# The last head's output weights: a quarter moved to two small loads, most of it on three DMA engines, ahead in the queue

## The chip, the cores and the metric

One core of a Trainium2 chip. The metric is the device time of one execution in microseconds (us), the median of several executions. Times inside an execution are counted from the start of the profiled span, which is some 1.7 us shorter than the device time.

A *row* below is one row of the output weights (512 bf16, 1 KB). The *rows step* is the group of small matmuls that reorders the attention outputs for the output product, and the *output matmuls* are those of that product. A *hole* is a stretch in which TensorE stands still with no semaphore to wait for. A *block* is 256 TensorE instructions: in the trace before, the holes end at instructions 450, 706, 962, 1218 and 1986, all multiples of 256 apart, with 0.4 to 1.1 us idle in each, and each ends 2.16 to 2.44 us after the start of an instruction packet of 16,384 B. At two more multiples, 1474 and 1730, there is no hole. *V4* is the load of the V rows of KV head 4; heads count from 0. An *increment* is one step of a load's semaphore, which counts up as the DMA engines of the load finish (the prediction reads it so; the load of V5 shows 16 of them in the trace before, from 55.51 to 57.26 us).

## The reference, cut to what matters

```python
# B=4 tokens, D=512, 32 query heads, 8 KV heads, head size 128, window of 1024 of 4096 positions
xn = layernorm(x)
q  = xn @ wq                                        # 512 x 4096
o  = softmax(q @ k.T * 128**-0.5) @ v               # per KV head: 1024 positions, 4 batches
s  = o.reshape(B, 1, 4096) @ wo                     # wo: 4096 x 512, 512 rows for each KV head
g  = silu(gelu(layernorm(xn) @ w1 + b1) @ w2 + b2)
return x + s * g
```

Almost everything is read once: 8 MB of K, 8 MB of V, 4 MB of each of wq and wo, 3.5 MB of MLP weights.

## The kernel before

All loads are issued in one queue, in the order in which they are used: wq and K, then V with the MLP weights between, then wo. What the change touches is at the end.

```python
wo_r = A_wo.rearrange("(g p i) o -> p g i o", g=HKV, i=4)   # head g: partition p holds 4 rows
for n, (g0, g1, i0, i1) in enumerate(((0, 2, 0, 4), (2, 4, 0, 4), (4, 6, 0, 4), (6, 7, 0, 4),
                                      (7, 8, 0, 3), (7, 8, 3, 4))):
    ...  # six loads; the last head's come as 3 + 1 rows of each partition

def to_rows(g0, g1):                  # 16 matmuls with selectors: OTb (head dim on partitions)
    ...                               # -> OW (rows on partitions, the order of the loads)
    t = add("pe", fn, ep[g1 - 1], c_sel, ex[HKV - 2])    # ep: the last head's epilogue
    return add("dve", ... OW[:, :, g0*4:g1*4] <- psx ..., t)

def wo(k, rows):                      # per head and row of the partition: 4 matmuls, 128 x 128 by 4
    ...
    last = pe.matmul(psM[:, PS_W + c * 4:PS_W + (c + 1) * 4],
                     wo_sb[:, g, i, c * 128:(c + 1) * 128], OW[:, i, g * 4:(g + 1) * 4], ...)
    return add("pe", fn, d, rows, mlp["g"])

for g in range(HKV):
    PV(g)                             # P times V on TensorE, then a matmul for the sums
    ...                               # epilogue(g - 1), parts of the MLP
epilogue(HKV - 1)
rows = to_rows(0, HKV)
for k in range(len(d_wo)):
    t_w = wo(k, rows)                 # 128 output matmuls; then product, transpose, sum, store
```

The softmax here doesn't subtract the row's maximum and nothing guards it: scores larger than these inputs give would overflow.

## Time and profile before

| Kernel before | |
|---|---|
| device time, median of 3 | 77.0 us (77.0 to 77.06) |
| profiled span | 75.3 us |
| bytes read | 28.85 MB |
| last increments of the last weights' semaphore | 72.17 us |
| hole among the output matmuls, from the last start before it to the next start | 69.38 to 70.13 us |
| product after the output matmuls starts | 72.52 us |

The prediction shows the lines that carry this. The table of stretches: stretch, its length, busy us and number of instructions of TensorE, its weight loads, VectorE, ScalarE and GpSimd, granted clock, DMA share, and in the last column GB/s.

```profile
52.00:54.00 2.00, 0.60 (x24) 0.53 (x21) 0.92 (x2) 0.98 (x2) 0.00 (x0) 0.90 1.00 422
54.00:56.00 2.00, 0.74 (x6) 0.46 (x6) 1.26 (x4) 0.00 (x0) 0.00 (x0) 0.50 1.03 434
56.00:58.00 2.00, 2.00 (x76) 2.00 (x76) 0.96 (x4) 0.18 (x1) 0.00 (x0) 0.50 1.02 430
```

### The profile page before, as it was taken

The page shows a single profiled execution, that of the slowest core. Times are in us where ns is not written, and L with a number is a line of the kernel's source. Part 1 is how long each engine was busy: PE and PEld are TensorE (multiplying, and loading weights), DVE is VectorE, ACT ScalarE, POOL GpSimd, SP SyncE. Part 2 cuts the span into 40 slices and gives each one's busy share as a digit, 9 for nine tenths or more (in the row PEclk, how much of TensorE's full clock was granted, in tenths as well). Part 3 has the DMA queues.
Part 4 walks back from the last instruction along what each step waited for, and adds up shares of the span by engine and source line. Part 5 has one row for each costly group of instructions (what it writes and reads, how often), then busy time and mean ns, then how long its engine had stood idle before and what let it go on. Part 6 is the DMA issues. An engine that isn't in the chain of part 4 may idle for free.

```text
span 75.3 us, 2297 instructions
## 1 busy us (share of the span) xinstructions
PE 50.0 (66%) x1046; PEld 39.8 (53%) x1058; DVE 39.3 (52%) x82; ACT 9.8 (13%) x16; POOL 4.6 (6%) x14
## 2 busy tenths in 40 slices
PE   0000039993859949987997994999069879818770
PEld 0000039992359939976997860104049576518740
DVE  0778107786058967985996424001664679770010
ACT  0611000000090303111130630003300000000000
POOL 6980000000000000000000000000000000000000
PEclk9999999999999999999999999569755555555555
DMA  1899999998999999999999999999999999999600
GB/s 36 244 455 405 420 422 479 435 444 370 427 422 431 422 418 431 427 414 466 401 420 453 406 443 390 427 431 409 427 427 440 418 401 416 418 420 416 252 25 2
DMA packets 4219, 28.99 MB, mean 385 GB/s; under 512 B 493, under 2 KB 625, under 8 KB 1650
## 3 DMA queue, kind: packets, MB, share of 16 engines
q1 hardware_dynamic: 4160, 28.84, 92.2%
q8 instruction: 8, 0.13, 0.6%
q10 hardware_dynamic: 50, 0.01, 0.1%
q14 instruction: 1, 0.01, 0.0%
HBM read 28.85 MB, written 0.00 MB: 383 GB/s over the span
## 4 chain that ended last, share of the span: by engine, by line
DMA 36%; PE 35%; SPq 16%; issue 5%; DVE 4%
DMA wo_sb<-in_A_wo_dram 24%; PE psK L278 22%; SPq L475 15%; DMA kv_buf<-in_A_k_cache_dram 12%; PE psS L297 7%; PE psO L362 3%; DVE kt_buf L284 2%; DVE q_sb L368 1%; PE psK L374 1%; PE psM L507 1%; PE psK L346 1%; PE psS L538 1%; SPq L212 1%; SPq L205 0%; DVE o_bf L540 0%
## 5 line engine op out<-in xcount | busy, mean ns | idle before, releaser
L278 PE MATMUL psK<-ident,kv_buf 128*128 128x128 bf16 x256 | 21.2, 237 | 11.8 <-DMA kv_buf<-in_A_k_cache_dram 10.6
L284 DVE COPY kt_buf<-psK 128x1024 bf16<-128x1024 bf16 x32 | 21.3, 691 | 8.7 <-PE psK L278 8.6
L278 PEld LDWEIGHTS psK<-ident,kv_buf 128*128 128x128 bf16 x256 | 17.1, 108 | 11.1 <-DMA kv_buf<-in_A_k_cache_dram 10.6
L297 PE MATMUL psS<-qT,kt_buf 128*128 128x16 bf16 x256 | 10.4, 169 | 1.7 <-issue 1.1
L297 PEld LDWEIGHTS psS<-qT,kt_buf 128*128 128x128 bf16 x256 | 9.4, 96 | 3.0 <-issue 2.1
L315 PEld LDWEIGHTS psO<-P_buf,kv_buf 128*128 128x128 bf16 x256 | 7.4, 102 | 3.0 <-issue 3.0
L315 PE MATMUL psO<-P_buf,kv_buf 128*128 128x16 bf16 x256 | 8.0, 173 | 1.0 <-DVE OTb L333 0.6
L328 DVE TENSOR_REDUCE den_sb<-psS 128x16 f32<-128x512 f32 x8 | 5.5, 691 | 4.2 <-PE psO L315 4.0
L305 ACT ACTIVATE P_buf<-psS 128x512 bf16<-128x512 f32 x8 | 4.8, 597 | 17.1 <-PE psS L297 17.1
L400 PE MATMUL psK<-w_sb,yT 128*32 128x512 bf16 x16 | 4.9, 1093 | 1.3 <-issue 1.3
L507 PE MATMUL psM<-OW,wo_sb 128*128 128x4 bf16 x128 | 3.9, 166 | 1.1 <-issue 0.6
L507 PEld LDWEIGHTS psM<-OW,wo_sb 128*128 128x128 bf16 x128 | 3.6, 104 | 1.4 <-issue 1.2
L411 DVE SCALAR_TENSOR_TENSOR kt_buf<-kt_buf,psK 128x512 f32<-128x512 f32 x1 | 0.7, 686 | 6.4 <-ACT kt_buf L410 6.4
L534 DVE TENSOR_TENSOR sg_sb<-psM,g_sb 128x16 f32<-128x16 f32 x1 | 0.2, 185 | 4.7 <-PE psM L507 4.7
L400 PEld LDWEIGHTS psK<-w_sb,yT 128*32 128x32 bf16 x16 | 0.5, 114 | 3.8 <-issue 3.8
L369 ACT ACTIVATE q_sb<-psO 128x512 bf16<-128x512 f32 x1 | 0.6, 597 | 13.5 <-PE psO L362 13.5
L424 PE MATMUL psK<-ident,kt_buf 128*128 128x128 bf16 x4 | 0.6, 307 | 2.4 <-DVE kt_buf L419 2.4
L331 DVE RECIPROCAL rden<-den_sb 128x16 f32<-128x16 f32 x8 | 2.0, 253 | 0.3
L362 PE MATMUL psO<-wq_sb,xT 128*32 128x512 bf16 x32 | 1.9, 380 | 0.3 <-DVE xT L351 0.3
L246 DVE CAST P_buf<-x_bf 4x512 f32<-4x512 bf16 x1 | 0.8, 795 | 2.4 <-DMA x_bf<-in_A_x_dram 2.4
L237 POOL TENSOR_SCALAR_AFFINE_SELECT negm<-zero_bf 128x512 bf16<-128x512 bf16 x1 | 1.9, 1852 | 0.1
L321 PE MATMUL psS<-P_buf,ones_bf 128*128 128x512 bf16 x3 | 1.8, 587 | 0.0
(64 smaller groups left out, 27.4 us busy)
## 6 DMA issues: line engine op xcount, KB each, us to landing
kv_buf<-in_A_k_cache_dram SPq DMA_DIRECT2D x8, 1024.0 KB, 19.9
kv_buf<-in_A_v_cache_dram SPq DMA_DIRECT2D x8, 1024.0 KB, 22.8
wq_sb<-in_A_wq_dram SPq DMA_DIRECT2D x2, 2048.0 KB, 11.3
w_sb<-in_B_w_dram SPq DMA_DIRECT2D x2, 1792.0 KB, 27.9
wo_sb<-in_A_wo_dram SPq DMA_DIRECT2D x3, 1024.0 KB, 24.3
wo_sb<-in_A_wo_dram SPq DMA_DIRECT2D x1, 512.0 KB, 21.5
wo_sb<-in_A_wo_dram SPq DMA_DIRECT2D x1, 384.0 KB, 18.2
wo_sb<-in_A_wo_dram SPq DMA_DIRECT2D x1, 128.0 KB, 18.0
```

The costliest lines, as they stand in the source:

```text
L237: c_neg = add("gp", lambda e: e.affine_select(negm[:, :], zero_bf[:, :], [[0, 32], [1, 4], [0, 4]], ALU.is_equal, NEG, base=0, channel_mul ...
L278: last = pe.transpose(psK[n % NB][:, j * 128:(j + 1) * 128], kv_buf[:, g, u * UT + j, :], ident[:, :])
L284: cp[n] = add("dve", lambda e: e.tensor_copy(kt_buf[:, n % NKT, :], psK[n % NB][:, 0:1024]), t, sc.get(n - NKT))
L297: last = pe.matmul(psS[g % 2][:, c * 16:(c + 1) * 16], kt_buf[:, n % NKT, j * 128:(j + 1) * 128], qT[:, g * 16:(g + 1) * 16], start=False, ...
L305: ex[g] = add("act", lambda e: e.activation(P_buf[:, g, :], psS[g % 2][:, 0:512], AF.Exp, scale=SCALE), sc[n])
L315: last = pe.matmul(pso[:, 0:16], kv_buf[:, (HKV + g) % NS, c, :], P_buf[:, g, c * 16:(c + 1) * 16], start=(c == 0), stop=(c == NC - 1))
L328: v = add("dve", lambda e: e.tensor_reduce(den_sb[:, cs], bass.AP(psS[g % 2], 0, [[512, 128], [1, 16], [16, NC]]), AX.X, ALU.add), den[g])
L331: v = add("dve", lambda e: e.reciprocal(rden[:, cs], den_sb[:, cs]), v)
L362: last = pe.matmul(psO[m // 4][32 * s:32 * s + 32, 0:512], xT[:, c, :], wq_sb[:, c, m * 512:(m + 1) * 512], start=(c == 0), stop=(c == 3), ...
L400: pe.matmul(psK[0][32 * s:32 * s + 32, 0:1024].bitcast(F32), yT[:, c, :], bass.AP(w1_sb, c * F + K0[s], [[4 * F, 128], [1, 4], [FC, 128]]) ...
L475: e.dma_start(wo_sb[:, g0:g1, i0:i1, :], wo_r[:, g0:g1, i0:i1, :]))))
L507: last = pe.matmul(psM[:, PS_W + c * 4:PS_W + (c + 1) * 4], wo_sb[:, g, i, c * 128:(c + 1) * 128], OW[:, i, g * 4:(g + 1) * 4], start=firs ...
```

## The change

Some DMA engines end the stream earlier than others, as the semaphores of the loads show (of the last weights' increments in the trace before, eight come by 70.73 us and eight from 71.37 to 72.17). The intent is to give three of the early engines more of the last head's weights and all the others less. So 120 of its 512 rows are loaded by a DMA on 24 partitions, which runs on three engines, and 8 rows by another on 8 partitions. Both come after V4 in the queue and go where the query weights lay. The other 384 rows stay in 128-partition loads. The new layout needs its own selectors, and 24 + 12 output matmuls in place of the last head's 16.

```diff
+    wox_sb = wq_sb[0:24, 0, 0:6 * D].rearrange("p (j o) -> p j o", j=6)
 ...                                    # selectors sel3 and selx, made by GpSimd
+        if g == 4:                     # in the loop over heads, behind load_v(4)
+            R3 = (7 * 512 + 384) * D
+            d_wox = [pg.dma("sp", "wox0", lambda e: e.dma_start(
+                wox_sb[:, 0:5, :].rearrange("p j o -> p (j o)"),
+                bass.AP(A_wo.tensor, R3, [[5 * D, 3], [15 * D, 8], [1, 5 * D]])), t_q),
+                pg.dma("sp", "wox1", lambda e: e.dma_start(
+                    wox_sb[0:8, 5, :], bass.AP(A_wo.tensor, R3 + 120 * D, [[D, 8], [1, D]])), t_q)]
 ...
-    (7, 8, 0, 3), (7, 8, 3, 4)                                # last head: 3 + 1 rows
+    w3_r = A_wo[7 * 512:7 * 512 + 384, :].rearrange("(p i) o -> p i o", i=3)   # 2 + 1 rows
 ...                                    # to_rows: 16 matmuls as before, for heads 0 to 6, and
+            for i in range(3):
+                for j in range(3):
+                    last = pe.matmul(psx[:, 128 + i * 4:132 + i * 4], sel3[:, j, i, :], ...)
+            for a in range(6):
+                last = pe.matmul(psx[0:24, 160 + a * 4:164 + a * 4], selx[:, a, :], ...)
 ...                                    # two more copies by VectorE: OW3, OWx
+        if n == 2:                     # after the third group of output matmuls
+            wo([(wox_sb[:, a, :], OWx[:, a * 4:(a + 1) * 4], False, False) for a in range(5)]
+               + [(wox_sb[0:8, 5, :], OWx[0:8, 20:24], False, False)], rows[2], *d_wox)
```

More of the change, by code (lines that the diff above doesn't have):

```diff
@@ L161, in bass_recurrent_scan__sliding_block_cached__mixer_channel_mlp__decode_kernel @@
     OW = sb([128, 4, HKV * 4], BF16)
+    sel3 = sb([128, 3, 3, 128], BF16)
+    selx = sb([128, 6, 24], BF16)
+    OW3 = sb([128, 12], BF16)
+    OWx = sb([24, 24], BF16)
     hT = sb([128, 64], BF16)
@@ L243, in bass_recurrent_scan__sliding_block_cached__mixer_channel_mlp__decode_kernel @@
         base=0, channel_multiplier=-1), c_o32)
+    ones_w = bass.AP(ones_bf, 0, [[128, 128], [0, 9], [1, 128]])
+    c_sel3 = add("gp", lambda e: e.affine_select(
+        sel3[:, :, :, :], ones_w, [[-128, 3], [1, 3], [3, 128]], ALU.is_equal, 0.0,
+        base=0, channel_multiplier=-1), c_1)
+    c_sx = add("gp", lambda e: e.affine_select(
+        selx[:, 0:5, :], ones_bf[:, 0:120], [[1, 5], [5, 3], [15, 8]], ALU.is_equal, 0.0,
+        base=0, channel_multiplier=-1), c_1)
+    c_sx5 = add("gp", lambda e: e.affine_select(
+        selx[:, 5, :], ones_bf[:, 0:24], [[1, 24]], ALU.is_equal, 0.0,
+        base=120, channel_multiplier=-1), c_1)
     v = add("dve", lambda e: e.tensor_copy(x32[:, :], x_bf[:, :]), d_x)
@@ L466, in bass_recurrent_scan__sliding_block_cached__mixer_channel_mlp__decode_kernel @@
         w2_sb[:, :, :], B_w2.rearrange("(p c) o -> p c o", c=FC)))
-    for g in range(2, HKV):
-        load_v(g)
-    wo_r = A_wo.rearrange("(g p i) o -> p g i o", g=HKV, i=4)
-    d_wo = []
-    for n, (g0, g1, i0, i1) in enumerate(((0, 2, 0, 4), (2, 4, 0, 4), (4, 6, 0, 4), (6, 7, 0, 4),
-                                          (7, 8, 0, 3), (7, 8, 3, 4))):
-        d_wo.append((g0, g1, i0, i1, pg.dma("sp", "wo%d" % n, lambda e, g0=g0, g1=g1, i0=i0, i1=i1:
-                                            e.dma_start(wo_sb[:, g0:g1, i0:i1, :],
-                                                        wo_r[:, g0:g1, i0:i1, :]))))
@@ L478, in to_rows @@
-    def to_rows(g0, g1):
-        psx = psS[0]
-        def fn(pe):
-            last = None
-            for i in range(4):
-                for j in range(4):
-                    last = pe.matmul(psx[32 * j:32 * j + 32, i * 32 + g0 * 4:i * 32 + g1 * 4],
-                                     sel[:, i, :],
-                                     bass.AP(OTb, g0 * 16 + j * 4,
-                                             [[HKV * 16, 128], [16, g1 - g0], [1, 4]]),
-                                     start=True, stop=True)
-            return last
-        t = add("pe", fn, ep[g1 - 1], c_sel, ex[HKV - 2])
-        return add("dve", lambda e: e.tensor_copy(
-            OW[:, :, g0 * 4:g1 * 4],
-            psx[:, 0:128].rearrange("p (i n) -> p i n", i=4)[:, :, g0 * 4:g1 * 4]), t)
@@ L497, in bass_recurrent_scan__sliding_block_cached__mixer_channel_mlp__decode_kernel @@
-    first = [True]
-    def wo(k, rows):
-        g0, g1, i0, i1, d = d_wo[k]
-        def fn(pe):
-            last = None
-            for g in range(g0, g1):
-                for i in range(i0, i1):
-                    for c in range(4):
-                        last = pe.matmul(psM[:, PS_W + c * 4:PS_W + (c + 1) * 4],
-                                         wo_sb[:, g, i, c * 128:(c + 1) * 128],
-                                         OW[:, i, g * 4:(g + 1) * 4],
-                                         start=first[0], stop=(k == len(d_wo) - 1 and i == i1 - 1),
-                                         skip_group_check=True)
-                        first[0] = False
-            return last
-        return add("pe", fn, d, rows, mlp["g"])
@@ L516, in bass_recurrent_scan__sliding_block_cached__mixer_channel_mlp__decode_kernel @@
-    for g in range(HKV):
+    for g in range(HKV):
+        if g >= 2:
+            load_v(g)
+        if g == 4:
[5 more added lines that the diff above has]
+                    wox_sb[0:8, 5, :], bass.AP(A_wo.tensor, R3 + 120 * D, [[D, 8], [1, D]])), t_q)]
@@ L528, in bass_recurrent_scan__sliding_block_cached__mixer_channel_mlp__decode_kernel, with load_wo @@
     epilogue(HKV - 1)
-    rows = to_rows(0, HKV)
-    for k in range(len(d_wo)):
-        t_w = wo(k, rows)
+    wo_r = A_wo.rearrange("(g p i) o -> p g i o", g=HKV, i=4)
+    d_wo = []
+    def load_wo(n, g0, g1, i0, i1):
+        d_wo.append((g0, g1, i0, i1, pg.dma("sp", "wo%d" % n, lambda e: e.dma_start(
+            wo_sb[:, g0:g1, i0:i1, :], wo_r[:, g0:g1, i0:i1, :]))))
+    for n, g0 in enumerate((0, 2, 4)):
+        load_wo(n, g0, g0 + 2, 0, 4)
+    load_wo(3, 6, 7, 0, 4)
+    w3_r = A_wo[7 * 512:7 * 512 + 384, :].rearrange("(p i) o -> p i o", i=3)
@@ new lines, in bass_recurrent_scan__sliding_block_cached__mixer_channel_mlp__decode_kernel, with to_rows, fn @@
+    d_w3 = [(i0, i1, pg.dma("sp", "w3%d" % i0, lambda e, i0=i0, i1=i1: e.dma_start(
+        wo_sb[:, 7, i0:i1, :], w3_r[:, i0:i1, :]))) for i0, i1 in ((0, 2), (2, 3))]
+    def to_rows():
+        psx = psS[0]
+        def fn(pe):
+            last = None
+            for i in range(4):
+                for j in range(4):
+                    last = pe.matmul(psx[32 * j:32 * j + 32, i * 28:(i + 1) * 28],
+                                     sel[:, i, :],
+                                     bass.AP(OTb, j * 4, [[HKV * 16, 128], [16, 7], [1, 4]]),
+                                     start=True, stop=True)
+            o = 7 * 16
+            for i in range(3):
+                for j in range(3):
+                    last = pe.matmul(psx[:, 128 + i * 4:132 + i * 4], sel3[:, j, i, :],
+                                     OTb[:, o + j * 4:o + j * 4 + 4],
+                                     start=(j == 0), stop=(j == 2))
+            for a in range(6):
+                last = pe.matmul(psx[0:24, 160 + a * 4:164 + a * 4], selx[:, a, :],
+                                 OTb[:, o + 12:o + 16], start=True, stop=True)
+            return last
+        t = add("pe", fn, ep[HKV - 1], c_sel, c_sel3, c_sx, c_sx5, ex[HKV - 2])
+        return [add("dve", lambda e: e.tensor_copy(
+            OW[:, :, 0:28], psx[:, 0:112].rearrange("p (i n) -> p i n", i=4)), t),
+            add("dve", lambda e: e.tensor_copy(OW3[:, :], psx[:, 128:140]), t),
+            add("dve", lambda e: e.tensor_copy(OWx[:, :], psx[0:24, 160:184]), t)]
@@ new lines, in wo, with fn @@
+    def wo(tiles, *deps):
+        def fn(pe):
+            last = None
+            for w, o, st, sp in tiles:
+                for c in range(4):
+                    last = pe.matmul(psM[:, PS_W + c * 4:PS_W + (c + 1) * 4],
+                                     w[:, c * 128:(c + 1) * 128], o,
+                                     start=(st and c == 0), stop=sp, skip_group_check=True)
+            return last
+        return add("pe", fn, *deps)
+    rows = to_rows()
+    for n, (g0, g1, i0, i1, d) in enumerate(d_wo):
+        wo([(wo_sb[:, g, i, :], OW[:, i, g * 4:(g + 1) * 4], n == 0 and g == 0 and i == 0, False)
+            for g in range(g0, g1) for i in range(i0, i1)], d, rows[0], mlp["g"])
+        if n == 2:
+            wo([(wox_sb[:, a, :], OWx[:, a * 4:(a + 1) * 4], False, False) for a in range(5)]
+               + [(wox_sb[0:8, 5, :], OWx[0:8, 20:24], False, False)], rows[2], *d_wox)
@@ L534, in bass_recurrent_scan__sliding_block_cached__mixer_channel_mlp__decode_kernel @@
+    for i0, i1, d in d_w3:
+        t_w = wo([(wo_sb[:, 7, i, :], OW3[:, i * 4:(i + 1) * 4], False, i == 2)
+                  for i in range(i0, i1)], d, rows[1])
     v = add("dve", lambda e: e.tensor_tensor(
```

## The prediction

> **What bounds the kernel now.** I read the page first, then the timeline of the last ten microseconds, the chain that ended last, the table of stretches, and last the trace's records of single packets and semaphore increments. Slices, queues and forms, from the page:
>
> ```profile
> PEclk9999999999999999999999999569755555555555
> DMA  1899999998999999999999999999999999999600
> ...
> q1 hardware_dynamic: 4160, 28.84, 92.2%
> q8 instruction: 8, 0.13, 0.6%
> ...
> L507 PE MATMUL psM<-OW,wo_sb 128*128 128x4 bf16 x128 | 3.9, 166 | 1.1 <-issue 0.6
> ```
>
> The DMA row is at nine tenths from 4 us to 70 us, so the kernel is one long stream of transfers (28.84 MB) with a tail. In the packet records the engines are rate bound: an 8,192 B packet takes 309 ns and the next begins 3 ns before its end, 306 ns apart. A megabyte load has eight such packets on each of 16 engines, 2.45 us, and the K loads land 2.45 us apart. The second thing to see is queue 8: eight instruction packets, all 16,384 B, at 25.5, 32.2, 38.3, 44.5, 50.5, 60.6, 67.8 and 71.7 us, each some 0.9 us long. They take time from one data engine at a time.
>
> The semaphore records show what this does. A load counts up as its 16 engines finish. Up to 25 us all increments of one load lie within 0.35 us. After that one more engine falls 1.2 to 1.4 us behind with each instruction packet. The last weight load counts 70.42, 70.47, 70.48, 70.51, 70.62, 70.64, 70.73, 70.73 and then 71.37, 71.82, ... 72.17: eight engines are early and eight late. I followed packets from end to start. The engine that alone carries the 3,584 B packet of b1, a one-row load, is never hit and writes its last data at 70.29 us. Two of the three others among the lowest four (those of the four-row b2 load) are not hit either. This is what the change wants to use.
>
> The end, from the timeline and then from the chain:
>
> ```profile
> 67.19 0.30 PE L486 MATMUL psS<-OTb,sel 128*32 128x32 bf16 x16 [1.30 <-DVE OTb L333]
> 67.56 0.29 DVE L493 CAST OW<-psS 128x128 bf16<-128x128 f32 x1 [0.42 <-PE psS L486]
> 68.00 1.55 PE L507 MATMUL psM<-OW,wo_sb 128*128 128x4 bf16 x53 [0.51 <-DVE OW L493]
> 70.13 2.35 PE L507 MATMUL psM<-OW,wo_sb 128*128 128x4 bf16 x75 [0.58 <-issue]
> 72.52 0.18 DVE L534 TENSOR_TENSOR sg_sb<-psM,g_sb 128x16 f32<-128x16 f32 x1 [4.67 <-PE psM L507]
> ```
>
> ```profile
> 53.69 18.16 DMA wo_sb<-in_A_wo_dram
> 71.86 0.05 issue
> 71.90 0.60 PE psM L507 x16
> ```
>
> The chain says that the load of the last head's first three rows of tiles ended the wait at 71.86 us, and 16 matmuls followed. But the timeline says that TensorE is almost as late. It makes 53 output matmuls, stands still with no semaphore to wait for ("issue") until 70.13 us, and makes 75 more. Single starts are 26.7 ns apart. The 112th matmul started at 71.68 us, so TensorE had only about 0.2 us of slack before the load that the chain blames. Of the 0.75 us hole the table of stretches shows:
>
> ```profile
> 69.40:70.13 0.73, 0.15 (x6) 0.09 (x4) 0.00 (x0) 0.00 (x0) 0.00 (x0) 0.50 1.03 411
> 70.13:71.70 1.57, 1.57 (x59) 1.57 (x58) 0.00 (x0) 0.00 (x0) 0.00 (x0) 0.50 0.50 191
> ```
>
> After the hole TensorE is full (1.57 of 1.57 us, 59 matmuls) while the DMA share has fallen to a half.
>
> I numbered TensorE's instructions in order, twice the weight loads plus the waits since some matmul records are missing. Holes without a releaser end at instructions 450, 706, 962, 1218 and 1986, all multiples of 256 apart. So the hole at 70.13 us is a block of instructions that had not arrived. Its packet began at 67.84 us and TensorE went on 2.29 us later; the four earlier pairs give 2.44, 2.22, 2.16 and 2.37 us.
>
> [...]one data increment for b1 (1 row), four for x and b2, eight for each half of x16. For a source of 3 by 8 rows and 24 partitions this gives three engines.
>
> **The change, part by part.** Transfers first. Packet durations are 46 ns for 1,024 B, 121 for 3,072, 159 for 4,096 and 309 for 8,192; a line through them gives 83 ns for 2,048 and 196 for 5,120 (estimates), each less the 3 ns of overlap.
> - Removed on every engine: 8 x 118 + 8 x 43 = 1.29 us for the last head. Added: 8 x 80 + 8 x 43 = 0.98 us for its 384 rows. Every engine ends 0.31 us earlier, the lowest eight 0.25 us because of a row of the small ninth load.
> - Added on the three lowest engines: 8 x 193 ns = 1.54 us plus 0.04. They end 1.3 us later than before, some 71.7 to 72.0 us in increments, level with the late ones.
> So the last weights should land at about 71.9 us instead of 72.17. By itself this is worth 0.2 to 0.3 us. The loads of V4 to V7 lose nothing: V7 landed at 62.11 us and its matmuls started at 64.45.
>
> TensorE next. Output matmuls become 28 x 4 + 6 x 4 + 3 x 4 = 148 instead of 128: 20 x 26.7 ns = 0.53 us more. The rows step grows from 16 to 31 matmuls; nine new ones load 128 columns and I take them at the same 26.7 ns, 0.24 us, the six of 24 columns at the old 7 ns, 0.04 us. So output matmuls begin at about 68.28 us. VectorE gets two more copies behind the first, needed only much later. GpSimd makes 1,152 + 144 more selector elements; 512 took 1.85 us, so about 4.7 us more, done by about 11 us and used at 67 us: free.
>
> Then the block boundary. It stays at instruction 1986, and what stands before the rows step is unchanged, so the boundary is 15 matmuls earlier in the output stage: after 38 of them rather than 53. TensorE gets there at 68.28 + 38 x 0.0267 = 69.29 us. [...]the packet still starts near 67.84 us and TensorE goes on at 70.13 us. This is my main choice: the hole swallows the 0.28 us of the rows step, but it now has 110 matmuls behind it instead of 75. 110 x 26.7 = 2.94 us, last start at 73.04 us, against 72.32 before: **0.72 us later**. The new load is there long before, the last weights at 71.9, so no DMA wait is left in that stretch. The tail (product, transpose, sum, store) is unchanged. The next boundary, 2242, is not reached: the program ends near 2211.
>
> **Rivals.**
> 1. The designer's: DMA sets the end, TensorE's matmuls hide, and 0.25 us is gained: 76.75 us. For it: the chain blames the load. Against: slack of only 0.2 us, and 35 more matmuls.
> 2. The block comes earlier[...], the hole closes. Then TensorE runs from 68.28 for 148 matmuls: last start at 72.20, gain 0.1 us: 76.9 us.
> 3. [...]the block comes some 0.3 us later, and the loss is 1.0 us: 78.0 us.[...]
> 4. An instruction packet falls on one of the three loaded engines, making it 1.2 us late: data at 73.2 us, 12 matmuls left, also about 1 us lost. One packet of eight matters here and three engines of 16, so unlikely.
>
> **Range and chances.** My main way gives 77.0 + 0.7 = 77.7 us; I give it two thirds, the two faster rivals a quarter together, the slower ones the rest. Middle 77.6 us, range 76.75 to 78.0. Two per cent is 1.54 us: no way named here reaches it, so 0.01 faster, 0.97 within, 0.02 slower.
>
> **What would show it.** Last weight increments near 71.9 us with the lowest engines no longer 1.4 us early; eight instruction packets again, the seventh near 67.8 us; a hole in the output matmuls after about 38, ending near 70.1 us; then 110 matmuls without a wait until about 73.1 us, and VectorE's product behind them rather than behind a load. The prediction is wrong if the hole ends before 69.8 us, if the seventh packet moves, or if matmuls at the end again wait for a load.

The sum came to 0.72 us more for the last output matmul, 77.0 + 0.7 = 77.7 us, with 77.6 us as the middle. But two of its inputs stand as my estimates alone: that the 24-partition load runs on three engines (the trace after then showed three data increments), and that the seventh packet still starts near 67.84 us (it started at 67.92). *Lowest* is my name for the engines that the small loads run on; no view numbers the engines, and that they lie one set inside the other was an estimate too. The trace after bears it out for the new loads: three of the eight 1 KB packets of the 8-row load start 1 to 2 ns after a 5 KB packet of the 24-partition load ends, at 54.48, 54.68 and 55.15 us. That the engine of b1 is never hit is my own following of packet records, in which several packets often fit as the next.

## The result and the profile after

The changed kernel took **77.94 us** (median of 4 runs, 77.68 to 78.04), against 77.03 us for the kernel before beside it. The ratio is 1.0114, 95% interval 1.0087 to 1.014. A ratio is always the mean time of one kernel's fast runs over that of the other's fast runs of the same rounds, so it is not quite the ratio of the medians.

The timeline of the changed kernel (start, length, engine, line, operation, count, and in brackets the idle time before it and what ended it):

```profile
67.14 0.30 PE L533 MATMUL psS<-OTb,sel 128*32 128x28 bf16 x16 [1.30 <-DVE OTb L351]
...
68.46 1.15 PE L559 MATMUL psM<-OW,wo_sb 128*128 128x4 bf16 x38 [0.46 <-DVE OWx L551]
70.26 1.71 PE L559 MATMUL psM<-OW,wo_sb 128*128 128x4 bf16 x58 [0.64 <-issue]
71.90 0.80 PE L559 MATMUL psM<-OWx,wq_sb 24*128 24x4 bf16 x24
72.62 0.91 PE L559 MATMUL psM<-OW,wo_sb 128*128 128x4 bf16 x28
```

The hole is now after 38 matmuls, ends at 70.26 us, and 58 + 24 + 28 = 110 matmuls follow. The chain that ended last says the same, and no load is left in its end:

```profile
69.62 0.64 issue
70.26 3.29 PE psM L559 x110
```

The queue is another matter. The same stretches as before:

```profile
52.00:54.00 2.00, 0.78 (x23) 0.48 (x19) 0.97 (x2) 0.93 (x2) 0.00 (x0) 0.85 1.00 410
54.00:56.00 2.00, 0.79 (x7) 0.51 (x8) 1.26 (x4) 0.00 (x0) 0.00 (x0) 0.50 1.01 319
56.00:58.00 2.00, 2.00 (x78) 2.00 (x78) 0.96 (x4) 0.18 (x1) 0.00 (x0) 0.50 1.03 434
```

From 54 to 56 us the engines are as busy as ever (1.01) but move 319 GB/s in place of 434. In the packet records, 8 KB packets that took 309 ns take up to 660 ns there, 58 of them between 53.4 and 56.1 us. All sixteen increments of V5's semaphore come later than before, the earliest at 56.15 us instead of 55.51, and the last weights land at 72.83 us instead of 72.17. The trace that I had predicted for TensorE was there. The loads, which I had expected to gain 0.25 us, had lost 0.66.

### The profile page after: what moved, and what is told of

Read it like the earlier page. It is cut to its first block, busy times and chain, and to the rows that moved or that the text cites. A ratio compares the mean times of both kernels' runs of the same rounds, so it can differ in the third digit from the quotient of the medians.

```text
span 76.3 us, 2387 instructions
## 1 busy us (share of the span) xinstructions
PE 52.7 (69%) x1093; PEld 40.8 (53%) x1093; DVE 39.3 (52%) x84; ACT 9.8 (13%) x16; POOL 6.5 (9%) x17
## 4 chain that ended last, share of the span: by engine, by line
PE 67%; DMA 12%; DVE 9%; issue 7%; ACT 2%; SPq 1%
PE psK L296 22%; DMA kv_buf<-in_A_k_cache_dram 12%; PE psO L333 8%; PE psS L315 8%; PE psK L418 6%; PE psM L559 6%; PE psS L339 4%; PE psO L380 3%; PE psS L311 3%; DVE kt_buf L302 2%; PE psM L460 2%; PE psK L422 1%; DVE q_sb L386 1%; DVE den_sb L346 1%; DVE kt_buf L437 1%
## 5 line engine op out<-in xcount | busy, mean ns | idle before, releaser
L339 PE MATMUL psS<-P_buf,ones_bf 128*128 128x512 bf16 x8 | 4.3, 534 | 0.0
L311 PE MATMUL psS<-negm,ind 128*128 128x512 bf16 x8 | 3.0, 380 | 0.0
```

Source lines behind the costliest of these rows:

```text
L311: pe.matmul(psS[g % 2][:, 0:512], ind[:, :], negm[:, :], start=True, stop=False, skip_group_check=True)
L339: den[g] = add("pe", lambda pe: pe.matmul(psS[g % 2][:, 0:512], ones_bf[:, :], P_buf[:, g, :], start=True, stop=True), ex[HKV - 2 + g % 2] ...
```

## The experiments

Each kernel ran on one chip beside the kernel before, and those of one batch on the same chip. Batch one: e1 to e4. Batch two: e5 to e7. Batch three: e8 to e10 and the changed kernel again. Last: e11.

| Run | What | Median, us | Range of its runs | Ratio to before | 95% interval |
|---|---|---|---|---|---|
| e1_tensor_alone | TensorE's added work only | 77.09 | 76.97 to 77.87 | 1.0014 | 0.9994 to 1.0034 |
| e2_loads_alone | loads only | 77.57 | 77.33 to 77.60 | 1.0071 | 1.005 to 1.0092 |
| e3_spread12 | small load over 12 engines | 77.72 | 77.57 to 78.28 | 1.0111 | 1.0069 to 1.0153 |
| e4_pad12 | 12 useless matmuls at the start | 77.72 | 77.49 to 77.86 | 1.0094 | 1.0068 to 1.0121 |
| e5_aligned | loads only, on partitions 0 to 11 and 32 to 43 (*aligned*) | 76.98 | 76.94 to 77.02 | 0.9998 | 0.9983 to 1.0013 |
| e6_no8rows | loads only, no 8-row load | 77.66 | 77.58 to 78.02 | 1.0096 | 1.0069 to 1.0122 |
| e7_later | loads only, placed after V7 | 77.46 | 77.38 to 77.70 | 1.0071 | 1.0048 to 1.0095 |
| e8_change_aligned | whole change, aligned | 77.28 | 77.11 to 78.08 | 1.0063 | 1.0024 to 1.0101 |
| e9_tensor_first | e8, reordered, with the pad | 77.08 (fast runs) | 76.92 to 77.66 | 1.0031 | 0.9999 to 1.0063 |
| e10_no_small_loads | loads only, 128 rows left out | 76.80 | 76.66 to 76.86 | 0.9971 | 0.9956 to 0.9986 |
| after_again | the changed kernel | 77.62 | 77.47 to 77.79 | 1.0083 | 1.0067 to 1.0099 |
| e11_balanced | repaired version | 76.74 | 76.62 to 76.81 | 0.9963 | 0.9949 to 0.9977 |

The kernel before had medians of 76.92 to 77.04 us in these batches. All runs were fast but one: e9's profiled execution (78.59 us) was slow and is left out of its row.

### TensorE's work alone (e1)

```diff
 # kernel before, its loads unchanged; in to_rows:
+            for a in range(9):  pe.matmul(psx[:, ...], ident[:, :], OTb[:, 112:116], ...)
+            for a in range(6):  pe.matmul(psx[0:24, ...], ident[:, 0:24], OTb[:, 124:128], ...)
 # and after the third group of output matmuls, adding exact zeros:
+                for a in range(20): pe.matmul(psM[:, ...], wo_sb[:, a // 4, 0, ...], zero_bf[:, 0:4], ...)
```

> The kernel before with all its loads as they were, and only TensorE's added work: 15 useless matmuls in the rows step (9 of 128 columns, 6 of 24), two more copies behind it, and 20 matmuls by zero after the third group of output weights. My theory (TensorE's tail behind the instruction block sets the end): as slow as the changed kernel, 77.8 to 78.1 us; the hole after about 38 output matmuls, ending near 70.2 us, and 110 matmuls behind it without a long wait; last weights still landing near 72.2 us. Rival (the loads on three engines slow the stream and set the end): no change, 77.0 to 77.2 us.

The profiled execution took 77.87 us and shows what I expected, by the chain:

```profile
68.48 1.16 PE psM L518 x38
69.64 0.66 issue
70.30 1.68 PE psM L518 x58
```

But the other four executions took 76.97, 76.98, 77.09 and 77.15 us, as fast as the kernel before. So with the added work one execution was 0.9 us slower and four were not. Only one trace of a run is kept, so no trace shows what was different in those four. The other traces do suggest it. In the traces of before, of after and of e1 the rows step starts at 67.19, 67.14 and 67.14 us; in those of e2, e3 and e4 below it starts at 65.71, 65.90 and 65.92 us. In those runs TensorE's holes of the K phase end earlier. The first hole, at instruction 450, ends at 27.94 us in after and at 26.28 us in e2, where the first instruction packet came at 24.0 and not at 25.7 us. I call the first kind executions with *late blocks* and the second kind with *early blocks*. They are the ends of a range and not two separate kinds: in the 13 traces of fast runs the first instruction packet starts between 21.55 us (after_again) and 25.69 us (after), with e7 at 25.00 and e8 at 25.12. That the four fast executions of e1 had early blocks is not shown.

### The loads alone (e2)

```diff
 # changed kernel; to_rows with 16 matmuls as before, 128 output matmuls:
-        if n == 2: wo([... the 24 matmuls of wox_sb ...], rows[2], *d_wox)
+        wo(group n == 3 also waits for *d_wox; their rows are multiplied nowhere)
+        4 matmuls by zero in place of the last head's fourth row
```

> The changed kernel's loads with TensorE's count of before (16 matmuls in the rows step, 128 output matmuls); the last 128 rows of weights are loaded but multiplied nowhere, so the result is wrong on purpose. My theory: the hole is back after 53 matmuls and ends near 70.2 us, so TensorE could end as before; the end follows the last weights. If these land at 72.8 us as in the changed kernel's trace, 77.5 us; if the slow stretch of packets near 54 us in that trace was chance, they land near 71.9 us and the time is 76.7 to 76.9 us. Rival (the loads alone cost the whole loss): 77.9 us.

The end is the loads', and the slow stretch was no chance. The chain, then the stretch:

```profile
55.64 16.55 DMA wo_sb<-in_A_wo_dram
72.18 0.05 issue
72.23 0.62 PE psM L534 x16
```

```profile
54.00:56.00 2.00, 1.85 (x66) 1.83 (x67) 1.14 (x4) 0.04 (x1) 0.00 (x0) 0.50 1.01 329
```

329 GB/s, last weights at 72.52 us, all four runs between 77.33 and 77.60. Here is a loss in every execution, and it belongs to the part of the change that was to bring the gain. The hole that I expected after 53 matmuls was not there, because this was an execution with early blocks.

### Twelve engines instead of three (e3)

```diff
-                bass.AP(A_wo.tensor, R3, [[5 * D, 3], [15 * D, 8], [1, 5 * D]])), t_q),
+                bass.AP(A_wo.tensor, R3, [[15 * D, 8], [5 * D, 3], [1, 5 * D]])), t_q),
```

> The changed kernel with the 120 rows in natural order, so that the load goes over 12 engines with two partitions each and not over three with eight. TensorE's work is the same. My theory: the same time as the changed kernel within 0.2 us (77.7 to 78.1), though the last weights should land near 72.3 us and not 72.8 if the packing on three engines caused the slow stretch of packets near 54 us. Rival (the three engines set the end): faster by 0.5 us or more.

The rows are now in natural order and the semaphore shows 12 data increments. The slow stretch remains:

```profile
54.00:56.00 2.00, 1.72 (x58) 1.59 (x58) 1.24 (x4) 0.00 (x0) 0.00 (x0) 0.50 1.04 353
```

The last weights landed at 72.59 us, not at 72.3, and the time is the changed kernel's. The packing on three engines is therefore not the cause of the slow stretch.

### Moving the block boundary (e4)

```diff
+    def f_pad(pe):
+        for _ in range(12): pe.matmul(psM[:, 0:4], ones_bf[:, :], ones_bf[:, 0:4], start=True, stop=True)
+    add("pe", f_pad, c_1)              # before the first transposes, where TensorE waits for K0
```

> The changed kernel with 12 useless matmuls (24 instructions) at the very start, where TensorE waits for the first K anyway. They move the block boundary 12 matmuls earlier in the output stage[...]. My theory: the seventh instruction packet starts near 67.0 us, the hole nearly closes (after about 26 matmuls, ending near 69.3 us), TensorE's last output matmul starts near 72.7 to 73.0 us, and the kernel is 0.3 to 0.6 us faster than the changed one, 77.3 to 77.6 us, for more work. Rival (the hole is no missing block[...]): 77.9 us or more.

A miss as a test. The trace is of an execution with early blocks: the seventh instruction packet starts at 64.79 us and there is no hole at all among the output matmuls. Yet 77.58 us remain, since TensorE then stands before the third group of weights until 70.51 us and has 84 matmuls behind it. The changed kernel shows the same without the pad (below). What the pad does where blocks come late, this run does not say.

### What slows the stream (e5, e6, e7)

The next guess was that it matters on which partitions the small load writes. In the changed kernel these are 24 in a row. I placed the same 120 rows on partitions 0 to 11 and 32 to 43, in two loads of twelve partitions, and the 8 rows on partitions 0 to 7 as before, in another order. I call this *aligned*. The reasons that I had for this choice, and for the theories of e5, e6 and e7, are not shown by any trace or run; they are cut from the expectations, and what stays of those is my estimate.

```diff
-                wox_sb[:, 0:5, :] <- bass.AP(A_wo.tensor, R3, [[5 * D, 3], [15 * D, 8], [1, 5 * D]])
-                wox_sb[0:8, 5, :] <- bass.AP(A_wo.tensor, R3 + 120 * D, [[D, 8], [1, D]])
+            for h in range(2):         # partitions 0 to 11 and 32 to 43
+                wox_sb[32 * h:32 * h + 12, 0:5, :] <- bass.AP(A_wo.tensor, R3 + h * 60 * D,
+                                                  [[5 * D, 3], [15 * D, 4], [1, 5 * D]])
+            wox_sb[0:8, 5, :] <- bass.AP(A_wo.tensor, R3 + 120 * D, [[D, 2], [2 * D, 4], [1, D]])
```

> The loads alone (result wrong on purpose, as in e2), but the small loads so placed[...]: partitions 0 to 11 and 32 to 43[...]. Theory[...]: the slow stretch near 54 us is gone, the last weights land near 71.9 us and the time is 76.6 to 76.9 us. Rival (what is slow lies on the source side or in a load on few engines as such): stretch as in e2, last weights near 72.5 us, 77.4 to 77.6 us.

```profile
52.00:54.00 2.00, 0.64 (x5) 0.38 (x5) 1.26 (x4) 0.00 (x0) 0.00 (x0) 0.50 1.01 424
54.00:56.00 2.00, 2.00 (x72) 1.98 (x73) 0.96 (x4) 0.18 (x1) 0.00 (x0) 0.50 1.03 436
```

The same 120 KB stand in the same place in the queue. I take them to go through three engines still: the sources are of 3 by 4 rows, and the changed kernel's of 3 by 8 rows had three data increments. The stretch is gone: 436 GB/s, the 8 KB packets of the stretch back at 309 ns, V5's first increment at 55.53 us. The small load's own 5 KB packets, up to 406 ns in the changed kernel, all take 196 ns. The time is that of the kernel before, not the 76.6 to 76.9 us that I expected. Thirteen increments of the last weights are in by 71.88 us, but the last three come at 72.00 to 72.12 us, later than the 71.9 of my expectation. I take them for the three loaded engines: they have become the last.

The next two kernels narrow it down further. e6 leaves out the 8-row load.

```diff
-                pg.dma("sp", "wox1", lambda e: e.dma_start(wox_sb[0:8, 5, :], ...
```

> The loads alone as in e2 but without the ninth load of 8 rows (its rows are left out; wrong on purpose). Theory[...]: the load on 24 partitions makes most of the stretch, so V5 still lands some 0.5 us late, the last weights near 72.4 us, 77.3 to 77.5 us. Rival (the eight rows on eight engines[...] do it): stretch gone, last weights near 71.9 us, 76.7 to 76.9 us.

```profile
54.00:56.00 2.00, 1.77 (x66) 1.72 (x65) 0.50 (x3) 0.18 (x1) 0.00 (x0) 0.50 1.02 317
```

317 GB/s, V5's first increment at 56.21 us, last weights at 72.72: the 24-partition load alone does it. e7 has both loads after V7.

```diff
-        if g == 4: d_wox = [...]       # behind V4
+    d_wox = [...]                      # behind V7, ahead of the other heads' output weights
```

> The loads alone as in e2, but the two small loads after V7, ahead of the output weights of the other heads. Theory[...]: the stretch moves there with its full size, near 61 to 63 us, and the end is as in e2, 77.4 to 77.6 us, while V5 and V7 land as in the kernel before. Rival (it is a matter of the V loads beside them): no stretch, last weights near 71.9 us, 76.7 to 76.9 us.

```profile
60.00:61.50 1.50, 1.22 (x46) 1.18 (x45) 1.09 (x4) 0.00 (x0) 0.00 (x0) 0.50 0.99 390
61.50:63.50 2.00, 1.89 (x55) 1.41 (x53) 1.82 (x5) 0.00 (x0) 0.00 (x0) 0.50 1.01 318
```

The kernel before, in the second of these stretches:

```profile
61.50:63.50 2.00, 1.77 (x46) 1.32 (x47) 1.55 (x4) 0.00 (x0) 0.00 (x0) 0.50 1.01 410
```

V5 lands as before (first increment at 55.57 us), and the stretch has moved to 61.5 to 63.5 us, 318 GB/s where the kernel before has 410, with its full cost: the last weights land at 72.57 us. It goes with the small load, not with what flows beside it.

What is shown: with a load of 24 consecutive partitions in this stream, every increment of the next V load comes 0.64 us later or more; the same bytes on 12 + 12 partitions cost none of this (V5's first increment at 55.53 us, for 55.51 before). In e11 below, 32 rows on 32 consecutive partitions leave no slow stretch either (441 GB/s from 54 to 56 us), so a run of consecutive partitions does not always bring it. e5 changed the partitions and also cut one load into two. A load that is split but not aligned, which would tell the two apart, was not run. Why the 24-partition load slows the stream is not shown.

### The whole change without the slow stretch (e8), and the changed kernel again

```diff
 # changed kernel with the loads of e5; selx and OWx on 44 partitions, the middle ones zero
```

> The whole change, correct, with the small loads aligned as in e5. Theory (two costs: the slow stretch of the stream in every execution, and TensorE's tail only where the instruction blocks come late): the stretch is gone, so executions with early blocks take 76.9 to 77.2 us and those with late blocks 77.7 to 78.0; mean ratio to before 1.001 to 1.007. Rival (TensorE's tail alone costs the loss): all executions near 77.7 to 78.0, ratio about 1.011.

Six executions: 77.11, 77.19, 77.28, 77.28 and then 77.94 and 78.08 us. These are the two clusters that were expected. The slower one is as slow as the changed kernel in its first trace (78.04 us), which had the slow stretch; no trace shows the blocks of these two. The retained trace (77.28 us) lies between the kinds: its rows step starts at 66.50 us, and the hole is there but ends early:

```profile
67.91 1.16 PE psM L563 x38
69.07 0.36 issue
69.44 3.38 PE psM L563 x110
```

The boundary is after the same 38 matmuls and the same 110 follow. Its end at 69.44 us instead of 70.26 accounts for the time.

> The changed kernel once more, for the spread of its executions beside the others and a second trace. Theory: 77.5 to 78.1 us, the faster ones with the rows step near 65.8 us and the end bound by the weights (the third group near 70.4 us, then 84 matmuls), the slower ones as in the first trace.

The changed kernel's second trace is one with early blocks (rows step at 65.85 us, seventh packet at 64.1 us, no hole):

```profile
44.66 25.77 DMA wo_sb<-in_A_wo_dram
70.44 0.04 issue
70.48 2.60 PE psM L559 x84
```

TensorE waits for the third group of weights, which the slow stretch has moved from 69.86 us (before) to 70.44, and then has 84 matmuls to do: 32 of the group, 24 of the small loads, 28 of the rest. Those of the small loads stand behind the wait although their weights had been there for 14 us. So even here the end is a sum of the two parts of the change. In this trace the product starts at 73.10 us, in the first at 73.57, before the change at 72.52.

### Taking the costs away (e9, e10, e11)

```diff
 # e9: e8, and the 24 matmuls of the small loads ahead of all other output matmuls, and e4's pad
 # e10: e2 without any small load: 128 rows are never read
```

> e8 with the 24 matmuls of the small loads ahead of all other output matmuls (their weights landed long before) and the 12 useless matmuls of e4 at the start. Theory: TensorE's tail is shortened in the executions with late blocks, so nearly all take 76.8 to 77.2 us, ratio 0.998 to 1.003; it can't be much below before, because the three engines now land last, near 72.1 us. Rival (the pad and the order do nothing): as e8.

Five fast runs, 76.92 to 77.66 us: three near 77.0, two near 77.6. The slower two are some 0.4 us faster than e8's slower two. Whether that is the edit is not shown: there is no trace of a fast run, and the run left out as slow is called so for its time alone (its granted clock, 0.829, is like that of the others). If it was one more execution with late blocks, the ratio flatters e9.

> e2 with the small loads left out altogether (128 rows of weights are never read; wrong on purpose): the most that unloading the other 13 engines could give. Theory: last weights near 71.85 us, no slow stretch, 76.6 to 76.8 us. If 77.0 us, even a perfect balance would have gained nothing.

76.80 us, last weights at 71.86 us, 0.31 us earlier than before, as the packets' sum had it. So there was something to gain from the loads alone, some 0.2 us, with TensorE's order as before.

e11 puts the parts together.

```diff
 # e9, with
+ 96 rows placed as in e5 (4 on a partition, partitions 0 to 11 and 32 to 43)
+ 32 rows on partitions 0 to 31, from a source of 8 by 4 rows
+ rows step of heads 0 to 6 right after head 6's epilogue, its copy on ScalarE,
+ and the first group of output matmuls there, where TensorE waits for the last epilogue
+ small-load matmuls after the second group
```

> A try at a version better than both, correct: aligned small loads with 96 rows on the three engines (4 on a partition) and 32 rows over eight engines; the rows of heads 0 to 6 and the first group of output matmuls before the last head's epilogue is done (the copy on ScalarE, which is idle there), small-load matmuls after the second group, and the 12 useless matmuls at the start. If both costs are understood: last weights near 71.9 us, TensorE no longer last, 76.75 to 77.0 us in most executions, ratio 0.996 to 1.000. If something else holds the end: 77.1 us or more.

That these loads run on three and on eight engines is estimated from the trace after, where the sources of 3 by 8 rows and of 8 rows had three and eight data increments.

76.74 us, all six runs within 0.19 us and no late cluster. It passed the check of the results, which proves little: e2, e5, e6, e7 and e10, which leave products of 128 rows out, are on record as correct too. From the timeline:

```profile
65.94 0.99 PE L567 MATMUL psM<-OW,wo_sb 128*128 128x4 bf16 x32 [0.48 <-ACT OW L574]
67.84 0.36 PE L557 MATMUL psS<-OTb,selx 128*44 128x4 bf16 x5 [0.67 <-issue]
71.03 1.24 PE L567 MATMUL psM<-OW,wo_sb 128*128 128x4 bf16 x28 [0.23 <-DMA wo_sb<-in_A_wo_dram]
```

The hole now lies in the rows step, from 67.0 to 67.8 us, and later TensorE waits for weights again. The last weights land at 71.95 us. It beats the kernel before by 0.37% (interval 0.23 to 0.51%). How much each of its edits gives was not separated.

## Why the prediction was right or wrong

**The total was right.** I gave 77.6 us and a range of 76.75 to 78.0 us; it took 77.94 (77.62 in the later batch), within 2% as I gave it. The way there was right in one half and wrong in the other.

**The block boundary: right.** The hole came after exactly 38 output matmuls. It ended at 70.26 us for the 70.13 predicted, with the seventh packet at 67.92 for 67.84, and 110 matmuls followed without a load among their waits. The output matmuls began 0.46 us later than before, not 0.28, which the hole swallowed as foreseen. The last began 3.11 us later and not 2.94: two pauses of some 0.09 us, where the matmuls of the small loads begin and end, are most of the difference. The packet's time did not move with the changed code, as I chose. GpSimd's selectors took 1.9 us more (4.6 to 6.5 us on the pages) and not 4.7, off the path.

**The transfers: wrong, and in sign.** The step that failed is "So the last weights should land at about 71.9 us instead of 72.17. By itself this is worth 0.2 to 0.3 us." They landed at 72.83. The packets removed were sized right: e10 measured their 0.31 us. That the three loaded engines were early ones was right as well: of the eight early increments of the last weights five are left (70.70 to 71.02 us in the trace after). The term that failed is that of the added load. I counted it as 1.54 us on three engines and nothing on the others, but V5's increments all came at least 0.64 us later. None of my rivals had a transfer that slows its neighbours. A smaller error lies beside it: without the slow stretch (e5) the last weights land at 72.12 us and not 71.9, so the balance itself was worth 0.05 us and not 0.27.

**"My main way" holds for the execution of the first trace, not for all.** I took the profile's times of the blocks for the kernel's. By my own signs of being wrong it fails in the second trace: there the seventh packet starts at 64.12 us, no hole is left, and the matmuls at the end wait for weights until 70.44 us. The missing block and the slow stretch do not add. In the first trace the loads, late as they are, are not on the chain, and e1's late execution took 77.87 us without the slow stretch against 78.04 with it. In the second trace the slow stretch moves the wait, and the 24 added matmuls lengthen what follows. That such executions also end at 77.5 to 77.8 us, near my 77.7, is luck. Which part is the larger in the mean is not settled: alone, TensorE's work cost 0.14% (e1) and the loads 0.71% (e2), the whole change without the slow stretch 0.63% with an interval of 0.24 to 1.01% (e8), and the whole change 0.83 to 1.14%.

**The rivals.** The designer's way (76.75 us) did not come: the slow stretch took the gain. e11 reached 76.74 us with other small loads and another order on TensorE. "The block comes earlier" is what the second trace shows, but its 76.9 us was not reached, because of the loads. No trace shows the other two.

**Open:** why the same kernel has its blocks earlier in one execution than in another, and the mechanism behind the slow stretch.

## What to carry to other kernels

Before giving work to DMA engines that look idle at the end, check what the new load does to the rest of the stream: one on 24 consecutive partitions took it from 434 to 319 GB/s for 2 us here, and GB/s at a full DMA share (1.01) shows it at once; the same bytes on 12 + 12 partitions, in two loads, did not (436 GB/s). Count instructions as well as time near the end of a long straight program: where a block boundary falls, and how many instructions stand behind it, can decide the tail (here 110 matmuls behind the hole in place of 75, and the product at 73.57 us in place of 72.52). Two costs on different paths need not add: here the missing block set the end in one trace and the late weights in the other. And a trace is one execution: compare its landmarks with a second one before taking its holes for the kernel's.
